# Last folds partly on GpSimd, six tiles' statistics on ScalarE, and a table of priorities in place of a search

## The chip, the core and the metric

The kernel runs on one core of a Trainium2 chip. The core has five engines that each work through a queue of their own in order: TensorE (PE in the profile; its weight loads are listed apart as PEld), VectorE (DVE), ScalarE (ACT), GpSimd (POOL) and SyncE (SP), which here issues all the loads and stores. The metric is the device time of one execution in microseconds. Three runs of the kernel before gave 236.53, 236.74 and 237.49 us; the median is 236.74.

## What is computed

```python
def reference(A_x, A_w_r, A_w_i, B_x, B_w_q, B_k1, B_k2, B_u, B_v):
    xn = layernorm(A_x)                              # (1, 2048, 576)
    # A: a filter in the frequency domain
    X = rfft2(xn) * (A_w_r + 1j * A_w_i)             # weights (2048, 289)
    yA = irfft2(X, s=(2048, 576))
    # B: experts picked by product keys, 32 heads, 8 x 8 experts, top 1
    q = einsum("nd,dhc->nhc", xn, B_w_q)             # w_q (576, 32, 256)
    s1 = einsum("nhd,ed->nhe", q[..., :128], B_k1)
    s2 = einsum("nhd,ed->nhe", q[..., 128:], B_k2)
    e = argmax(s1) * 8 + argmax(s2)
    act = gelu(einsum("nd,nhd->nh", xn, B_u[e]))
    yB = einsum("nh,nhd->nd", act, B_v[e])           # softmax over one is 1
    return A_x + yA + yB
```

## The kernel before

The 2048 rows are kept as 16 tiles of 128 rows (row 16n + t is in tile t), all in `XN`. The work falls into stages, each a small Python function marked `@staged`:

- `ln` takes the mean and the variance of each row of a group of tiles with VectorE's `bn_stats` (two passes of 288 numbers, into `st`) and `bn_aggr` (into `mv`), and makes the factors `rr` from them. `folds` adds and subtracts mirrored columns (GpSimd into the tile called `t` in the profile, GpSimd and VectorE into `A`) and makes `Rs`, the constant matrix times the row factor, on ScalarE. `dft128` multiplies by `Rs` on TensorE and copies the result out of PSUM as two 16 bit halves, the high one on ScalarE, the rest on VectorE, into `AB` and `ABL`.
- The spectral stages run for 16 groups g: `d_fwd` (transform along the columns, result in `A`), `s_fwd` and `s_inv` (the rest of the row transform and its inverse, with constants `s` loaded by `load_s16`), and between them `s_mul`, in which VectorE multiplies by the weights `Wt` with a scale `wx`, GpSimd makes `y`, and ScalarE and GpSimd its halves `yh`. `load_w` loads `Wt` and has ScalarE sum its absolute values into `wm` (tile `wa`). `w_scale` gets the scale from these sums.
- `allmax` takes the maximum of a column over all 128 partitions, for up to four columns: TensorE transposes, VectorE reduces (`mxr`), VectorE puts the maxima on a diagonal (`mxd`), and TensorE multiplies `ones` by it, which hands the maxima to all partitions. It runs nine times: in `w_scale` seven times, in `uv_prep` and in `fold_scale`.
- `fold_part` multiplies the loaded `wq` by the keys (`w` by `KP` on TensorE, 32 loads of 576 KB), `fold_end` makes `MU` and `MUL` of it. `x_t` normalises a tile again, splits it in halves `hl` and transposes it by DMA into `xT`. `scores`, `route` and `combine` take the scores (`MU` by `xT`), pick the experts on VectorE, and leave coefficients in `CAT`.
- The tail has 16 tiles t. `d_inv(t)` transforms back along the columns into a PSUM tile `p` of two blocks of 290. ScalarE copies the second half of each block, scaled, into `qs`; VectorE adds it to the first half (128x2x145) and subtracts it from it (128x2x144) into `eo` (the profile's `t`); GpSimd adds and subtracts the two blocks of `eo` into `y` (the profile's `A`, two instructions, 289 and 287 numbers). `fin(t, y)` multiplies by the constant `RT` and adds the experts' part (`vS`) on TensorE, VectorE adds the input, and SyncE stores.

The functions only record their instructions. A planner, `_Plan`, then sets the order in which they are issued on every engine: it runs through the recorded instructions with assumed durations (`cost`), takes on each engine the ready one with the highest priority (`forward`), and a priority is the assumed length of the work that hangs on an instruction (`backward`) plus a bias (`plan.base` or `plan.bias` at the time of recording). Before, ten rounds of that are followed by 1500 tries with random shifts of the priorities by stage, and the order with the shortest assumed time is kept. All instructions are issued from one line (L487), so the profile names them by tiles. PSUM tiles get their banks in the same way; all other tiles come from rings of buffers.

Of the kernel before, what the change touches and what calls it, by code (L numbers as in the profile page):

```python
# [135 lines left out]
TRIES, SEED = 1500, 2  # L136
# [87 lines left out]
class _Plan:  # L224
# [7 lines left out]
    def cost(self, eng, m, out, ins, kw):  # L232
# [4 lines left out]
        if eng == "sync":  # L237
            return out.shape[0] * n * size_of(out.dtype) / 400.0 + (2500 if kw.get("transpose") else 0), self.land
# [111 lines left out]
    def forward(self, prio):  # L350
# [50 lines left out]
        best, stale = dict.fromkeys(free), set(free)  # L401
        while len(order) < len(ops):
            for e in best:
                if e in stale:
# [16 lines left out]
            if o.opens:
                new = [v for v in o.opens if v not in slot]
                for v, k in zip(new, banks(new)[1]):
                    slot[v] = k
                    free_at[k:k + v.banks] = [INF] * v.banks
                    used[v.kind] += 1
                stale.add("tensor")
            for v in o.tiles:
                left[v] -= 1
                end[v] = max(end[v], free[e] + o.lat)  # L430
                if not left[v]:
                    free_at[slot[v]:slot[v] + v.banks] = [end[v]] * v.banks
# [8 lines left out]
        return max(free.values()), order, slot, start

    def issue(self):
# [16 lines left out]
        for _ in range(ROUNDS):  # L460
# [7 lines left out]
        for k in range(TRIES):
            f = 1 - k / TRIES
            tail, shift = cur[1], cur[2].copy()  # L470
            pick = rng.random(len(shift)) < (0.02, 0.05, 0.15)[rng.integers(3)]
            shift[pick] += rng.normal(0, 800 + 4000 * f, pick.sum())
            more = 400 * f * f * rng.exponential()
            if k % 40 == 39:
                tail, shift, more = self.backward(got[3]), cur[2], 300
            new = self.forward([t + o.bias + shift[o.stage] for t, o in zip(tail, ops)])
            if new[0] <= cur[0] + more:
                cur, got = (new[0], tail, shift), new
                if new[0] < best[0]:
                    best = new  # L480
# [18 lines left out]
def _body(ctx, tc, nc, plan, a, out):  # L499
# [238 lines left out]

    @staged
    def w_end():  # L740
# [247 lines left out]

    @staged
    def d_inv(t):  # L990
        p = PS("a")
        for b in range(2):
            P.matmul(p[:, b, :290], ABLt[:99, b, :, t], il[:99, b, :], start=True, stop=False)
            for c in range(2):
                cs = slice(0, 145) if b == c else slice(145, 290)
# [152 lines left out]
```

## Time and profile before

| | |
|---|---|
| median of three runs | 236.74 us |
| the profiled execution | 237.5 us |
| its span in the trace | 235.6 us |
| granted clock of TensorE, mean | 0.986 |
| read from HBM | 38.33 MB |

The profile is of one execution. Its span runs from the first to the last instruction that the profiler recorded; the execution itself took 1.9 us longer. Busy time is the time in which an engine executes; an engine that waits in its queue is idle, and the profile names what ended the wait. For groups of instructions a row gives the engine, the operation, output and inputs by tile, shapes, the count, the busy time, the mean duration in ns, and the idle time ahead of them.

### The profile page before, as it was taken

To read this page: it belongs to the slowest core of one execution; us is meant where nothing else is said; L and a number is where in the kernel's file an instruction comes from. 1 tells how busy PE (TensorE), PEld (TensorE's weight loads), DVE (VectorE), ACT (ScalarE), POOL (GpSimd) and SP (SyncE) were. 2 spreads that over 40 slices of the span, in tenths; PEclk is the share of its full clock that TensorE was granted. 3 is DMA by queue.
4 is the path that set the end of the run, shared out by engine and by line. 5 is a ranking of instruction groups with operands and counts; after the bars stand their busy time and mean duration, and the time that the engine had idled before them with its cause. 6 is when DMAs were issued, how large, how long until landed. Compare 5 with 4: busy or idle time off the path is not lost.

```text
span 235.6 us, 5937 instructions
## 1 busy us (share of the span) xinstructions
PE 200.0 (85%) x2271; PEld 135.8 (58%) x2271; DVE 204.3 (87%) x446; ACT 125.9 (53%) x287; POOL 134.4 (57%) x183
## 2 busy tenths in 40 slices
PE   0466888998999877899988979689999999999893
PEld 0454657776566545774454566265546778767661
DVE  2789999995999679976499999989999999968992
ACT  2232658989789599989635665256432121223120
POOL 2978768984264446736228886275813746545340
PEclk9997999999999999999999999979999999999999
DMA  6999999999999998466525561330521357662175
GB/s 211 401 403 415 362 334 375 406 349 373 284 338 374 392 251 148 106 164 59 110 53 122 115 134 38 79 59 3 100 59 46 99 156 253 198 203 100 50 245 208
DMA packets 34252, 48.15 MB, mean 204 GB/s; under 512 B 20784, under 2 KB 23088, under 8 KB 33840
## 3 DMA queue, kind: packets, MB, share of 16 engines
q1 hardware_dynamic: 34224, 47.77, 64.7%
q8 instruction: 18, 0.29, 0.6%
q14 instruction: 10, 0.08, 0.1%
HBM read 38.33 MB, written 4.72 MB: 183 GB/s over the span
## 4 chain that ended last, share of the span: by engine, by line
DVE 45%; PE 29%; ACT 9%; issue 8%; DMA 7%; POOL 1%; DVEq 0%; ACTq 0%; POOLq 0%
PE banks L487 29%; DVE w L487 9%; DVE t L487 8%; DVE AB L487 5%; DVE A L487 3%; DVE st L487 3%; DMA Wt<-in_W_dram 3%; DMA w<-in_x_dram 3%; DVE v L487 2%; DVE cw L487 2%; ACT AB L487 2%; DVE mx L487 2%; DVE ABL L487 2%; DMA XN<-in_x_dram 2%; DVE rr L487 2%
## 5 line engine op out<-in xcount | busy, mean ns | idle before, releaser
L487 POOL TENSOR_TENSOR A<-t 128x145 f32<-128x145 f32 (+3 forms) x56 | 38.4, 706 | 18.9 <-DVE t L487 12.2
L487 PE MATMUL banks<-MU,xT 128*128 128x512 f16 x192 | 46.0, 380 | 0.0
L487 PE MATMUL banks<-c,AB 128*128 128x145 f16 (+1 forms) x384 | 35.6, 228 | 0.7 <-DVE AB L487 0.7
L487 PEld LDWEIGHTS <-AB 128*128 128x128 f16 x384 | 31.6, 121 | 6.7 <-issue 4.3
L487 PE MATMUL banks<-Rs,A 128*128 128x128 f32 x128 | 20.5, 310 | 16.1 <-ACT Rs L487 11.8
L487 POOL TENSOR_TENSOR y<-t,t 128x289 f32<-128x289 f32 x32 | 21.7, 700 | 21.2 <-DVE t L487 20.8
L487 PEld LDWEIGHTS <-xT 128*128 128x128 f16 x224 | 19.8, 97 | 23.7 <-issue 4.1
L487 POOL TENSOR_TENSOR yh<-y,yh 128x578 f16<-128x578 f32 x16 | 20.6, 1285 | 16.7 <-ACT yh L487 12.9
L487 PEld LDWEIGHTS banks<-Rs,A 128*128 128x128 f32 x128 | 17.7, 214 | 21.1 <-ACT Rs L487 14.1
L487 POOL TENSOR_TENSOR t<-XN 128x289 f32<-128x289 f32 x32 | 24.5, 782 | 8.2 <-DMA XN<-in_x_dram 3.8
L487 DVE TENSOR_TENSOR AB<-banks,AB 128x512 f16<-128x512 f32 x32 | 21.6, 676 | 5.2 <-ACT AB L487 2.7
L487 DVE SCALAR_TENSOR_TENSOR t<-banks,wx,Wt 128x578 f32<-128x578 f32 x32 | 24.9, 807 | 0.4 <-PE banks L487 0.3
L487 POOL TENSOR_TENSOR hl<-XN,hl 128x576 f16<-128x576 f32 x16 | 20.0, 1254 | 8.0 <-ACT hl L487 8.0
L487 PE MATMUL banks<-c,ABL 99*128 99x289 f16 (+1 forms) x64 | 18.7, 292 | 5.6 <-DVE t L487 2.7
L487 ACT ACTIVATE yh<-banks,sc 128x290 f32<-128x290 f32 x16 | 8.0, 503 | 27.9 <-PE banks L487 23.9
L487 PE MATMUL banks<-A,c 128*128 128x288 f32 x64 | 21.6, 419 | 0.5 <-DVE t L487 0.5
L487 PE MATMUL banks<-w,KP 128*32 128x288 f32 x256 | 21.2, 428 | 0.0
L487 ACT ACTIVATE ABL<-banks 99x256 f16<-99x256 f32 x32 | 12.1, 378 | 16.6 <-PE banks L487 15.8
L487 ACT ACTIVATE AB<-banks 128x512 f16<-128x512 f32 x32 | 18.9, 590 | 0.1
L487 PE MATMUL banks<-s,yh 64*128 64x128 f16 x384 | 14.5, 222 | 4.9 <-ACT yh L487 1.9
L487 DVE TENSOR_TENSOR ABL<-banks,ABL 33x256 f16<-33x256 f32 x32 | 13.0, 405 | 6.3 <-ACT ABL L487 3.2
L487 PEld LDWEIGHTS <-yh 64*128 64x128 f16 x384 | 11.6, 97 | 9.6 <-issue 3.5
(104 smaller groups left out, 416.5 us busy)
## 6 DMA issues: line engine op xcount, KB each, us to landing
w<-in_wq_dram SPq DMA_DIRECT2D x32, 576.0 KB, 6.2
Wt<-in_W_dram SPq DMA_DIRECT2D x16, 289.0 KB, 5.4
w<-in_x_dram SPq DMA_DIRECT2D x8, 576.0 KB, 4.3
out_dram<-w SPq DMA_DIRECT2D x16, 288.0 KB, 2.7
XN<-in_x_dram SPq DMA_DIRECT2D x3, 1282.0 KB, 12.7
s<-in_s_dram SPq DMA_DIRECT2D x16, 192.0 KB, 3.1
XN<-in_x_dram SPq DMA_DIRECT2D x2, 641.0 KB, 5.0
c<-in_c_dram SPq DMA_DIRECT2D x1, 868.5 KB, 7.5
```

The costliest lines, as they stand in the source:

```text
L487: fn(*[x.place() if isinstance(x, _Ps) else x for x in args], **{k: x.place() if isinstance(x, _Ps) else x for k, x in kw.items()})
```

## The change

Five things are changed.

1. `d_inv`: for all 16 tiles ScalarE copies both halves of the blocks (`es`, 2x290 numbers instead of 2x145), and the subtraction moves from VectorE to GpSimd, which reads both inputs from SBUF. VectorE's addition stays.
2. `ln`: for the tiles 5, 7, 9, 11, 13 and 15 ScalarE takes the statistics, in one pass with a sum for the mean and one pass with a sum of squares for the variance; GpSimd scales the mean. `bn_stats` and `bn_aggr` go for these.
3. `allmax`: the diagonal goes; the maxima, broadcast along their row, are the weights of the second product, with the identity as what moves. A factor can be put into the last instruction, so a separate scaling in `w_scale` and one in `fold_scale` go.
4. The planner: the 1500 tries go; a table `SHIFT` of one number per stage is added to the priorities instead. Its assumed times change: 1200 ns until a transposing load lands instead of 3000, 3000 instead of 5600 for the early loads, and 2600 more for a load that is issued when the queue has been full for over 1500.
5. The spectral stages get a bias (`plan.base`) of 1e4 instead of 0.

```diff
-TRIES, SEED = 1500, 2
+SHIFT = (
+    43015, -9167, -18816, 63625, -68848, 40186, 12971, -53665, -16763, -54647, 23343, -31988,
...
+)
@@ cost
-            return out.shape[0] * n * size_of(out.dtype) / 400.0 + (2500 if kw.get("transpose") else 0), self.land
+            return out.shape[0] * n * size_of(out.dtype) / 400.0 + (2500 if kw.get("transpose") else 0), 1200.0 if kw.get("transpose") else self.land
@@ forward
+            lag = 0.0
+            if e == "sync":
+                if t0 > full[1]:
+                    full[0] = t0
+                full[1] = free[e] + 300
+                lag = 2600.0 if t0 - full[0] > 1500 else 0.0
             for k, lat in o.after:
-                ready[k] = max(ready[k], free[e] + lat)
+                ready[k] = max(ready[k], free[e] + lat + lag)
@@ issue
-        rng = np.random.default_rng(SEED)
-        for k in range(TRIES):
...
+        best = self.forward([t + o.bias + SHIFT[o.stage] for t, o in zip(cur[1], ops)])
@@ allmax
-        dg = T([4, 4], F32, "mxd", 4)
-        V.tensor_scalar(dg[:k, :k], idn[:k, :k], m[:k, 0:1], None, op0=OP.mult)
-        P.matmul(p[:, 1, :k], ones[:k, :], dg[:k, :k], start=True, stop=True)
-        V.tensor_scalar(dst, p[:, 1, :k], 1e-10, None, op0=OP.max)
+        P.matmul(p[:, 1, :k], m[:k, 0:1].to_broadcast([k, 128]), idn[:k, :k], start=True, stop=True)
+        if up is None:
+            V.tensor_scalar(dst, p[:, 1, :k], 1e-10, None, op0=OP.max)
+        else:
+            V.tensor_scalar(dst, p[:, 1, :k], 1e-10, up, op0=OP.max, op1=OP.mult)
@@ ln
+            if t + i in SA:
+                j, b = T([128, D], BF, "wa", 1), rr[:, 3, t + i:t + i + 1]
+                A.activation(j, XN[:, t + i, 64:64 + D], AF.Copy, scale=-1.0 / 13824, accum_out=b)
+                A.activation(j, XN[:, t + i, 64:64 + D], AF.Square, scale=1.0 / 24, bias=b, accum_out=mv[:, i, 1:2])
+                G.tensor_scalar(mv[:, i, 0:1], b, -24.0, None, op0=OP.mult)
+                continue
@@ w_scale
-        V.tensor_scalar(wx[:, 1, g:g + n], wx[:, 1, g:g + n], 2.0 ** -12, None, op0=OP.mult)
@@ d_inv
+            es = T([128, 2, 290], F32, "qs", 2, "yh")
+            A.activation(es, p[:, :, 0:290], AF.Copy, scale=sc[:, 12:13])
+            qs = es[:, :, 145:290]
...
-        V.scalar_tensor_tensor(eo[:, :, 288:144:-1], p[:, :, 0:144], sc[:, 12:13], qs[:, :, 0:144],
-                               op0=OP.mult, op1=OP.subtract)
+            G.tensor_tensor(eo[:, :, 288:144:-1], es[:, :, 0:144], qs[:, :, 0:144], op=OP.subtract)
```

What the order does with it shows at three places. The first is ScalarE in the first stage, from its second instruction for `rr` on, before:

```order
L487 ACTIVATE rr_84<-mv_1_94,eps_85 128x2
L487 ACTIVATE yl_0_103<-A2_0_97 128x198
L487 ACTIVATE ABL_76<-banks_66 99x64x4
L487 ACTIVATE AB_75<-banks_66 128x128x4
L487 ACTIVATE yl_0_103<-A2_2_99 128x198
L487 ACTIVATE rr_84<-mv_0_93,eps_85 128x4
L487 ACTIVATE Rs_0_101<-c32_68,rr_84 128x128
L487 ACTIVATE Rs_1_102<-c32_68,rr_84 128x128
```

and of the change, where `wa<-XN` are the two passes of a tile's statistics (the first one's sum goes to `rr`, the second one's to `mv`):

```order
L502 ACTIVATE rr_84<-mv_1_94,eps_85 128x2
L502 ACTIVATE ABL_76<-banks_66 99x64x4
L502 ACTIVATE yl_0_103<-A2_0_97 128x198
L502 ACTIVATE wa_0_105,rr_84<-XN_67 128x576
L502 ACTIVATE wa_0_105,mv_0_93<-XN_67,rr_84 128x576
L502 ACTIVATE AB_75<-banks_66 128x128x4
L502 ACTIVATE wa_0_105,rr_84<-XN_67 128x576
L502 ACTIVATE Rs_0_101<-c32_68,rr_84 128x128
L502 ACTIVATE wa_0_105,mv_0_93<-XN_67,rr_84 128x576
L502 ACTIVATE yl_0_103<-A2_2_99 128x198
L502 ACTIVATE rr_84<-mv_0_93,eps_85 128x4
L502 ACTIVATE Rs_1_102<-c32_68,rr_84 128x128
```

The passes of tiles 5 and 7 stand ahead of the copy `AB` and between the two `Rs`. The second place is ScalarE in the spectral stages, at the sum `wa` over the weights of group 6, whose buffer is `Wt_2`, before:

```order
L487 ACTIVATE A2_2_99<-banks_66 128x578
L487 ACTIVATE yl_0_103<-yh_0_142 128x198
L487 ACTIVATE wa_0_114,wm_82<-Wt_2_110 128x578
L487 ACTIVATE yh_1_143<-y_0_141 128x578
L487 ACTIVATE AB_75<-banks_66 128x4x128
L487 ACTIVATE yl_1_104<-yh_1_143 128x198
```

and of the change:

```order
L502 ACTIVATE AB_75<-banks_66 128x4x128
L502 ACTIVATE yh_1_139<-y_0_137 128x578
L502 ACTIVATE ABL_76<-banks_66 99x2x128
L502 ACTIVATE yl_1_104<-yh_1_139 128x198
L502 ACTIVATE wa_0_105,wm_82<-Wt_2_111 128x578
L502 ACTIVATE yl_1_104<-yh_1_139 128x198
```

The sum has moved behind `AB`, `yh` and `ABL`. SyncE's queue shows the load that it needs. Before, from that load to the last one of `wq`:

```order
L487 DMA Wt_2_110<-in_W_dram 128x578
L487 DMA s16_1_116<-in_s16_dram 128x768
L487 DMA w_4_131<-in_wq_dram 128x1152
L487 DMA Wt_3_111<-in_W_dram 128x578
L487 DMA w_0_127<-in_wq_dram 128x1152
L487 DMA w_1_128<-in_wq_dram 128x1152
```

and of the change:

```order
L502 DMA Wt_2_111<-in_W_dram 128x578
L502 DMA w_1_124<-in_wq_dram 128x1152
L502 DMA s16_1_116<-in_s16_dram 128x768
L502 DMA Wt_3_112<-in_W_dram 128x578
L502 DMA w_3_126<-in_wq_dram 128x1152
L502 DMA Wt_4_113<-in_W_dram 128x578
L502 DMA s16_2_117<-in_s16_dram 128x768
L502 DMA Wt_5_114<-in_W_dram 128x578
L502 DMA w_0_123<-in_wq_dram 128x1152
L502 DMA w_4_127<-in_wq_dram 128x1152
L502 DMA w_1_124<-in_wq_dram 128x1152
L502 DMA w_2_125<-in_wq_dram 128x1152
```

Three of the 32 loads of `wq` stood behind it, now six do. The third place is the end of GpSimd's queue, the last four tiles' folds and two `chl` of `combine`, before:

```order
L487 TENSOR_TENSOR A2_0_97<-t1_0_95 128x289
L487 TENSOR_TENSOR A2_1_98<-t1_1_96 128x287
L487 TENSOR_TENSOR A2_1_98<-t1_1_96 128x289
L487 TENSOR_TENSOR A2_2_99<-t1_0_95 128x289
L487 TENSOR_TENSOR A2_2_99<-t1_0_95 128x287
L487 TENSOR_TENSOR chl_0_151<-ca_0_150,chl_0_151 128x2x64
L487 TENSOR_TENSOR A2_3_100<-t1_1_96 128x289
L487 TENSOR_TENSOR A2_3_100<-t1_1_96 128x287
```

and of the change, where `t1<-yh` is the moved subtraction:

```order
L502 TENSOR_TENSOR t1_0_95<-yh_0_138 128x2x144
L502 TENSOR_TENSOR A2_0_97<-t1_0_95 128x289
L502 TENSOR_TENSOR A2_0_97<-t1_0_95 128x287
L502 TENSOR_TENSOR chl_0_147<-ca_0_146,chl_0_147 128x2x64
L502 TENSOR_TENSOR t1_1_96<-yh_1_139 128x2x144
L502 TENSOR_TENSOR A2_3_100<-t1_1_96 128x289
L502 TENSOR_TENSOR t1_0_95<-yh_0_138 128x2x144
L502 TENSOR_TENSOR A2_3_100<-t1_1_96 128x287
L502 TENSOR_TENSOR A2_2_99<-t1_0_95 128x289
L502 TENSOR_TENSOR A2_2_99<-t1_0_95 128x287
```

Each tile has three instructions there instead of two, and the subtraction of the last tile stands ahead of the last addition of the tile before it.

More of the change, by code (lines that the diff above doesn't have):

```diff
@@ L400, in forward @@
         order, start = [], [0.0] * len(ops)
-        best, stale = dict.fromkeys(free), set(free)
+        best, stale, full = dict.fromkeys(free), set(free), [0.0, 0.0]
         while len(order) < len(ops):
@@ L465, in issue @@
                 best = got
-                cur = got[0], tail, np.zeros(self.stage + 1)
-        rng = np.random.default_rng(SEED)
-        for k in range(TRIES):
[L469 to L480, printed above, removed]
+                cur = got[0], tail
+        best = self.forward([t + o.bias + SHIFT[o.stage] for t, o in zip(cur[1], ops)])
         _, order, slot, start = best
@@ L550, in _body @@
     plan.bias = 8e6
-    plan.land = 5600.0
+    plan.land = 3000.0
     c32 = K([128, 3, 128], F32, "c32")
@@ L614, in allmax @@
     @staged
-    def allmax(src, k, dst):
+    def allmax(src, k, dst, up=None):
         p = PS("m", (128, 2, 256))
@@ L734, in w_scale @@
     def w_scale(g, n):
-        allmax(wm[:, g:g + n], n, wx[:, 0, g:g + n])
+        allmax(wm[:, g:g + n], n, wx[:, 0, g:g + n], 4096.0)
         V.reciprocal(wx[:, 1, g:g + n], wx[:, 0, g:g + n])
-        V.tensor_scalar(wx[:, 1, g:g + n], wx[:, 1, g:g + n], 2.0 ** -12, None, op0=OP.mult)
     @staged
@@ L743, in w_end @@
         V.tensor_reduce(sc[:, 12:13], al, axis=AX, op=OP.add)
-        V.tensor_scalar(sc[:, 12:13], sc[:, 12:13], 4.0 / 1179648.0, sc[:, 10:11], op0=OP.mult, op1=OP.mult)
+        V.tensor_scalar(sc[:, 12:13], sc[:, 12:13], 4.0 / 1179648.0 / 4096.0, sc[:, 10:11], op0=OP.mult, op1=OP.mult)
     mt = {}
@@ L986, in s_inv @@
         V.tensor_tensor(lo[:33], lv[:33], lo[:33], op=OP.subtract)
+    EG = range(16)
     @staged
@@ L998, in d_inv @@
                              stop=(c == 1 and n == 2))
-        qs = T([128, 2, 145], F32, "qs", 2, "yh")
-        A.activation(qs, p[:, :, 145:290], AF.Copy, scale=sc[:, 12:13])
         eo = T([128, 2, L], F32, "eo2", 2, "t1")
-        V.scalar_tensor_tensor(eo[:, :, 0:145], p[:, :, 0:145], sc[:, 12:13], qs, op0=OP.mult, op1=OP.add)
-        V.scalar_tensor_tensor(eo[:, :, 288:144:-1], p[:, :, 0:144], sc[:, 12:13], qs[:, :, 0:144],
-                               op0=OP.mult, op1=OP.subtract)
+        if t in EG:
+            es = T([128, 2, 290], F32, "qs", 2, "yh")
+            A.activation(es, p[:, :, 0:290], AF.Copy, scale=sc[:, 12:13])
+            qs = es[:, :, 145:290]
+        else:
+            qs = T([128, 2, 145], F32, "qs", 2, "yh")
+            A.activation(qs, p[:, :, 145:290], AF.Copy, scale=sc[:, 12:13])
+        V.scalar_tensor_tensor(eo[:, :, 0:145], p[:, :, 0:145], sc[:, 12:13], qs, op0=OP.mult, op1=OP.add)
+        if t in EG:
+            G.tensor_tensor(eo[:, :, 288:144:-1], es[:, :, 0:144], qs[:, :, 0:144], op=OP.subtract)
+        else:
+            V.scalar_tensor_tensor(eo[:, :, 288:144:-1], p[:, :, 0:144], sc[:, 12:13], qs[:, :, 0:144],
+                                   op0=OP.mult, op1=OP.subtract)
         y = T([128, D], F32, "yy", 2, "A2")
@@ L1067, in _body @@
     scores(0)
+    plan.base = 1e4
     for g in range(4):
@@ L1074, in _body @@
     for g in range(16):
+        plan.base = 1e4
         s_inv(g)
@@ L1081, in _body @@
             load_s16(g + 4)
-            plan.base = 0
+            plan.base = 1e4
             if g % 2 == 1:
@@ L1088, in _body @@
                 w_scale(g + 3, 2)
+        plan.base = 0
         r = g // 2
@@ L1100, in _body @@
             combine(r)
+    plan.base = 0
     w_end()
```

4 lines of the change are left out of this document (2 added, 2 removed), and 18 rows, old and new, of the table SHIFT.

## The prediction

> **What bounds the kernel now.** I read the share table first, then the stretches by engine, then the waits of TensorE.
>
> ```profile
> PE 200.0 (85%) x2271; PEld 135.8 (58%) x2271; DVE 204.3 (87%) x446; ACT 125.9 (53%) x287; POOL 134.4 (57%) x183
> DVE 45%; PE 29%; ACT 9%; issue 8%; DMA 7%; POOL 1%; DVEq 0%; ACTq 0%; POOLq 0%
> 0.00:10.00 10.00, 1.05 (x5) 1.06 (x6) 5.33 (x23) 2.55 (x5) 5.52 (x17) 1.00 0.82 288
> 10.00:40.00 30.00, 22.90 (x182) 17.12 (x182) 27.70 (x89) 14.69 (x42) 23.53 (x39) 0.94 0.99 381
> 40.00:80.00 40.00, 38.21 (x554) 27.00 (x552) 36.11 (x75) 34.21 (x77) 25.06 (x31) 1.00 1.00 358
> 80.00:100.00 20.00, 15.81 (x276) 11.10 (x275) 15.82 (x36) 17.81 (x39) 10.62 (x12) 1.00 0.88 195
> 100.00:180.00 80.00, 72.14 (x888) 43.54 (x887) 71.42 (x131) 45.80 (x101) 42.75 (x49) 0.98 0.40 84
> 180.00:232.00 52.00, 49.88 (x379) 36.00 (x377) 47.37 (x96) 10.81 (x25) 26.95 (x38) 1.00 0.47 160
> 232.00:235.60 3.60, 0.00 (x0) 0.00 (x0) 0.52 (x1) 0.00 (x0) 0.00 (x0) 1.00 0.43 168
> ```
>
> The stretches give, after the stretch and its length, busy us of PE, PEld, DVE, ACT and POOL, the granted clock, the DMA share and GB/s. Two engines are nearly full, VectorE with 204.3 us and TensorE with 200.0 of a span of 235.6. The chain that ended last (the second row) runs mostly over VectorE, because TensorE work is in order and waits for it. But TensorE cannot go below its 200.0 us, and the change takes next to nothing off it. So the span is 200.0 plus the 35.6 us in which TensorE idles, and the question is how much of that idle time VectorE causes. By stretch, length less busy time: 8.95 in the first 10 us, 7.10 in 10 to 40, 1.79 in 40 to 80, 4.19 in 80 to 100, 7.86 in 100 to 180, 2.12 in 180 to 232, and 3.60 at the end, together 35.6. The first and the last (12.55) are the first load, the first normalisation and the last output; the change does not touch them. That leaves 23.06.
>
> ```profile
> PE banks L487 <- DVE A L487: 3.4, 3, 2.3
> PE banks L487 <- ACT Rs L487: 2.8, 2, 2.2
> PE banks L487 <- DVE rr L487: 0.9, 1, 0.9
> ...
> 81.25 0.69 ACT L487 ACTIVATE wa<-Wt 128x578 bf16<-128x578 f32 x1 [2.27 <-DMA Wt<-in_W_dram]
> ...
> PE banks L487 <- ACT yh L487: 1.9, 1, 1.9
> PE banks L487 <- DVE t L487: 1.9, 2, 1.6
> PE banks L487 <- DVE wx L487: 1.3, 1, 1.3
> ```
>
> The first three rows are all waits of TensorE from 10 to 40 us (total, times, longest): 7.1 us, all on the normalisation and the folds, `Rs` too, since it is `rr`, written by VectorE, times a constant. The 4th row is ScalarE at 81 us, held 2.27 us by a load of `Wt`, with `yh` and `AB` queued behind it. The last three are the longest waits from 100 to 180 us; VectorE is 71.42 of 80 us busy there.
>
> **The change, part by part: VectorE.** These rows (count, then busy us and the mean ns of one) are what goes:
>
> ```profile
> L487 DVE SCALAR_TENSOR_TENSOR t<-banks,sc,yh 128x288 f32<-128x288 f32 x16 | 8.0, 502 | 0.0
> L487 DVE BATCH_NORM_STATS2 st<-XN 128x6 f32<-128x288 f32 x32 | 12.2, 442 | 3.7 <-DMA XN<-in_x_dram 3.7
> L487 DVE BATCH_NORM_AGGREGATE mv<-st 128x2 f32<-128x12 f32 x16 | 2.0, 171 | 0.0
> L487 DVE TENSOR_SCALAR mxd<-c,mxr x9: 193/753/1101, 50.9 to 136.1; 2x2 f32<-2x2 f32 x7, 4x4 f32<-4x4 f32 x1, 1x1 f32<-1x1 f32 x1
> L487 DVE TENSOR_SCALAR mxd<-c,mxr 2x2 f32<-2x2 f32 x7 | 4.3, 618 | 0.1
> L487 DVE TENSOR_SCALAR mxd<-c,mxr 4x4 f32<-4x4 f32 x1 | 0.8, 804 | 0.0
> L487 DVE TENSOR_SCALAR mxd<-c,mxr 1x1 f32<-1x1 f32 x1 | 0.2, 193 | 0.0
> L487 DVE TENSOR_SCALAR wx<-wx 128x2 f32<-128x2 f32 x6 | 3.4, 560 | 0.1
> L487 DVE TENSOR_SCALAR wx<-wx x7: 151/170/1190, 53.6 to 140.8; 128x2 f32<-128x2 f32 x6, 128x4 f32<-128x4 f32 x1
> ```
>
> The second half of the last folds: 16 times 0.502 is 8.0 us. Six tiles' statistics: 12 of 32 passes at 12.2/32 and 6 of 16 aggregates at 2.0/16 make 4.6 and 0.75, so 5.3. The diagonals `mxd`: 4.3 + 0.8 + 0.2, so 5.3. The scalings of `wx`: 3.4 for six and 0.17 for one; one of `sc` at the same 0.17. Together 22.3 us, so VectorE falls from 204 to about 182 and is no longer beside TensorE.
>
> A diagonal of four numbers takes 0.193 us at best and 1.101 at worst, and `wx` 0.151 and 1.190: most of it is waiting. [...]
>
> **ScalarE and GpSimd** get work:
>
> ```profile
> L487 ACT ACTIVATE wa<-Wt 128x578 bf16<-128x578 f32 x16 | 10.9, 682 | 2.5 <-DMA Wt<-in_W_dram 2.3
> L487 ACT ACTIVATION_READ_ACCUMULATOR wa<-Wt 128x1 f32 x16 | 3.1, 195 | 0.0
> L487 ACT ACTIVATE yh<-banks,sc 128x290 f32<-128x290 f32 x16 | 8.0, 503 | 27.9 <-PE banks L487 23.9 <-DVE v L487 3.3 <-ACT MT L487 0.7
> L487 ACT ACTIVATE A<-banks 128x578 f16<-128x578 f32 x16 | 10.3, 654 | 5.3 <-PE banks L487 5.3
> L487 POOL TENSOR_TENSOR y<-t,t 128x289 f32<-128x289 f32 x32 | 21.7, 700 | 21.2 <-DVE t L487 20.8
> L487 POOL TENSOR_TENSOR A<-t 128x287 f32<-128x287 f32 x16 | 13.2, 827 | 10.0 <-DVE t L487 4.0 <-DVE w L487 2.8 <-DVE pw L487 2.2
> L487 POOL TENSOR_TENSOR A<-t 128x289 f32<-128x289 f32 x16 | 12.0, 757 | 8.2 <-DVE t L487 8.2
> L487 POOL TENSOR_SCALAR rr<-mv 128x2 f32<-128x2 f32 x2 | 0.5, 270 | 0.2
> ```
>
> A pass over 576 numbers with a sum is the nearest to `wa`: 0.682 + 0.195 = 0.88 us, 12 of them 10.5 us on ScalarE. The copy of 580 numbers out of PSUM instead of 290 is nearest to `A`: 0.654 against 0.503, so 16 times 0.15, 2.4 us. ScalarE goes from 125.9 to about 139. GpSimd gets 16 subtractions of 288 numbers: bounds 0.70 (the row of `y`) and 0.83 (the slowest of the tail's rows), I take 0.70, 11.2 us; and six small scalings at 0.27, 1.6 us. It goes from 134 to 147. The new subtraction waits for the copy of ScalarE, and behind it in GpSimd's queue stand the additions `y` of the tile before, for which TensorE's last products wait. Per tile the chain was 0.503 + 0.508 + 0.502 on ScalarE and VectorE; now it is 0.654 and then 0.508 beside 0.70, so 0.16 us shorter, and the PSUM bank comes free earlier, since the subtraction reads SBUF.
>
> The weights broadcast from `m` have no row. `ones` has the same shape, so I take a difference of nothing; bounds of 0.1 us either way for 9 of them, from the 0.183 us load of `ones` and the 0.082 of two columns elsewhere, are under 1 us.
>
> ```profile
> L487 PEld LDWEIGHTS banks<-mxd,ones 2*128 2x128 f32 x14 | 2.1, 183 | 2.4 <-DVE mxd L487 1.2 <-DVE wx L487 0.8 <-issue 0.2
> L487 PEld LDWEIGHTS banks<-c,wm 128*2 128x2 f32 x6 | 0.5, 82 | 2.1 <-DVE t L487 0.9 <-ACT wa L487 0.8 <-issue 0.2
> ```
>
> **From busy time to the span.** 10 to 40 us: of the 7.10 idle, 3.87 lies before 20 us (the stretch of 10 to 20 below), on tiles 0 to 4, whose statistics stay. Of the other 3.2 I take 2.0: VectorE, 27.70 of 30 busy, loses 5.3 us there, and the new passes lie on ScalarE, which has 15 us free, but in front of evacuations (first pair of order pieces above).
>
> ```profile
> 10.00:20.00 10.00, 6.13 (x37) 4.60 (x36) 7.90 (x28) 2.75 (x8) 8.02 (x14) 1.00 1.01 405
> ```
>
> 40 to 80 us: the DMA share is 1.00, TensorE waits 1.8; nothing. 80 to 100 us: 4.2 idle, of which I take 2.0: the load of `Wt` that ScalarE waited for now has six of the 32 loads of `wq` behind it and not three, and its `wa` stands behind `AB` and `yh` (second and third pair of order pieces); one load of 576 KB is 1.5 us at the 381 GB/s of a full stretch, so it lands some 4 us earlier than the 2.27 us wait needs. If another load is late there instead, the 2.0 stay. 100 to 180 us: VectorE is 89% busy, and what it sheds here (`mxd`, `wx`, and tail work that no longer presses) is about a tenth; I take half of 7.86, 4.0, since its waits on `yh` of ScalarE and GpSimd stay. 180 to 232 us: TensorE is 49.88 of 52 busy. The 8.0 us that go from VectorE lie under that; nothing. Sum: 2.0 + 2.0 + 4.0 = 8.0 off 235.6, a span of 227.6. The profiled execution took 237.5, 1.9 more than its span; the median shown, 236.74, is 0.76 below it. So 227.6 + 1.9 - 0.76 = **228.7 us**.
>
> **The rivals.**
> *Everything frees up.* All 23.06 less the 3.87 before 20 us goes, 19.2: 217.5 us. Against it: waits on ScalarE and DMA are not touched by VectorE's relief. Taken at 218 to 224, chance 0.07.
> *A small gain.* The new priorities only reshuffle the waits of 100 to 180 us, and 2 to 4 us come off: 233 to 235. For it: the waits there are scattered over five releasers. Chance 0.20.
> *The statistics block ScalarE*, so that the change doesn't do what it says. Each of the 12 passes stands in the queue of the copies `AB`, `ABL` and `Rs`; if each pair holds TensorE for one pass, 6 times 0.88 is 5.3 us, against 2.0 + 4.0 won elsewhere: 236.0, within half a per cent, which is about what a measurement can tell from no change. For it: ScalarE is 34.21 of 40 busy right after. Against: the loads of `wq` give TensorE other work. Chance 0.12.
> *GpSimd paces the tail* (the slower one). Per tile it now does three instructions, 0.70 + 0.757 + 0.827 = 2.28 us, with 2.6 us of others in all (26.95 less 25.2) 2.4 per tile; TensorE needs 49.88/16 = 3.1. It decides from a mean of 0.98 us per instruction. The longest of the first folds (row below) is 1.192; at that all through, 16 times 3.7 is 59.8, 9.9 more than TensorE, and 236.7 - 6 + 9.9 = 240.6. Chance 0.09.
>
> ```profile
> L487 POOL TENSOR_TENSOR t<-XN x32: 687/788/1192, 4.8 to 49.7; 128x289 f32<-128x289 f32 x32
> L487 DVE TENSOR_TENSOR A<-t 128x288 f32<-128x288 f32 x8 | 3.5, 436 | 0.0
> L487 POOL TENSOR_TENSOR A<-t 128x288 f32<-128x288 f32 x8 | 6.2, 773 | 0.1
> ```
>
> [...]
>
> **How the numbers follow.** The forecast, 224 to 233 us, has 0.52. Faster by over 0.5%: 0.52 + 0.20 + 0.07 = 0.79; within it 0.12; slower 0.09. A range of 221 to 238 leaves out the slower rival (0.09), half of the one that frees everything, and a little of the others.
>
> **What would show it.** Right: VectorE near 182 us, TensorE still 200, idle of TensorE near 27.5, and in the tail no wait of TensorE on GpSimd. The statistics: ScalarE passes near 0.88 us and waits of TensorE from 20 to 40 us under 1.5. Wrong: GpSimd above nine tenths in the tail, evacuations late behind `wa`, or a new long wait for a load at 55 to 90 us, since `Wt` and the c16 constants changed places in the queue.

## The result, and the profile after

Four runs of the changed kernel have a median of 228.89 us (228.73 to 231.18); four of the kernel before beside them 236.63 (236.34 to 237.49). The ratio is 0.969, with a 95% interval of 0.962 to 0.976: faster by 3.1%. The prediction was 228.7. Here and below, a time is the median of all runs of a kernel, and ratios, intervals and mean clocks leave out the slow runs, those over 1.5% above the fastest of the same kernel. The profiled execution of the changed kernel is its slowest run, 231.18 us with a span of 229.4, so the profiles differ by 6.2 us of span and the medians by 7.7.

The page of the changed kernel first, its busy times and the shares of the chain that ended last; then the stretches (stretch, length, busy us of PE, PEld, DVE, ACT and POOL, granted clock, DMA share, GB/s):

```profile
PE 197.8 (86%) x2271; PEld 135.6 (59%) x2271; DVE 189.6 (83%) x395; ACT 136.5 (60%) x311; POOL 147.5 (64%) x205
PE 44%; DVE 25%; ACT 11%; DMA 8%; issue 8%; POOL 3%; DVEq 0%; ACTq 0%; POOLq 0%
0.00:10.00 10.00, 0.73 (x3) 0.73 (x4) 5.37 (x22) 2.64 (x5) 5.45 (x16) 1.00 0.81 277
10.00:40.00 30.00, 24.18 (x199) 17.85 (x197) 25.38 (x77) 23.15 (x68) 26.84 (x48) 0.94 1.01 408
40.00:80.00 40.00, 37.25 (x566) 27.34 (x562) 31.71 (x68) 35.19 (x79) 24.98 (x31) 1.00 0.98 320
80.00:100.00 20.00, 16.10 (x283) 11.47 (x274) 11.86 (x28) 17.49 (x40) 8.46 (x9) 0.91 0.84 240
100.00:180.00 80.00, 76.70 (x917) 46.56 (x916) 75.43 (x134) 46.69 (x101) 49.64 (x58) 1.00 0.43 90
180.00:226.00 46.00, 42.81 (x327) 31.69 (x324) 39.88 (x71) 11.38 (x21) 32.17 (x47) 1.00 0.52 174
226.00:229.40 3.40, 0.00 (x0) 0.00 (x0) 0.00 (x0) 0.00 (x0) 0.00 (x0) 0.93 0.23 87
```

The chain now runs over TensorE first (44%) and VectorE second (25%); before it was 29 and 45. TensorE's idle time, stretch by stretch as the prediction counted it (length less busy time):

| stretch, us | idle before | idle after | predicted change | measured |
|---|---|---|---|---|
| 0 to 10 | 8.95 | 9.27 | 0 | +0.3 |
| 10 to 40 | 7.10 | 5.82 | -2.0 | -1.3 |
| 40 to 80 | 1.79 | 2.75 | 0 | +1.0 |
| 80 to 100 | 4.19 | 3.90 | -2.0 | -0.3 |
| 100 to 180 | 7.86 | 3.30 | -4.0 | -4.6 |
| 180 to the end | 5.72 | 6.59 | 0 | +0.9 |
| idle in all | 35.6 | 31.6 | -8.0 | -4.0 |
| TensorE busy | 200.0 | 197.8 | 0 | -2.2 |

The order differs, so a stretch doesn't hold exactly the same work; the sums don't depend on that. One thing already speaks against a step of the prediction: from 100 to 180 us VectorE is *busier* than before, 75.43 us instead of 71.42, and it is just there that TensorE waits less.

What TensorE still waits for, by releaser, from 10 to 40 us and (last three) from 100 to 180 us (total, times, longest):

```profile
PE banks L502 <- DMA w<-in_wq_dram: 3.7, 4, 1.7
PE banks L502 <- ACT Rs L502: 2.0, 2, 1.1
...
PE banks L502 <- DVE t L502: 1.6, 4, 0.6
PE banks L502 <- POOL chl L502: 1.4, 1, 1.4
PE banks L502 <- DVE AB L502: 0.3, 1, 0.3
```

The waits on the folds (`A`, 3.4 us) are gone from the front, and a wait for the loads of `wq` has come, at a DMA share of 1.01. From 100 to 180 us the three largest totals of before, 1.9, 1.9 and 1.3 us, are now 1.6, 1.4 and 0.3. The timeline from 80 to 100 us has two waits of TensorE of over 0.3 us (start, duration, instruction, in brackets the wait). Three rows of ScalarE and VectorE, of the same stretch, stand under them:

```profile
85.90 0.38 PE L502 MATMUL banks<-c,wm 128*2 128x128 f32 x2 [2.09 <-DVE A L502]
95.58 0.27 PE L502 MATMUL banks<-c,mm__90 128*1 128x128 f32 x1 [1.44 <-ACT hl L502]
...
83.73 0.69 ACT L502 ACTIVATE wa<-Wt 128x578 bf16<-128x578 f32 x1
84.42 0.63 ACT L502 ACTIVATE A<-banks 128x578 f16<-128x578 f32 x1
85.08 0.76 DVE L502 TENSOR_TENSOR A<-banks,A 128x578 f16<-128x578 f32 x1 [1.83 <-ACT A L502]
```

The groups of the changed kernel that are new or altered (count, busy us, mean ns of one, idle ahead and its releaser):

```profile
L502 ACT ACTIVATE yh<-banks,sc 128x580 f32<-128x580 f32 x16 | 11.9, 744 | 27.8 <-PE banks L502 23.5 <-POOL act L502 3.3 <-issue 1.0
L502 POOL TENSOR_TENSOR t<-yh 128x288 f32<-128x288 f32 x16 | 11.8, 734 | 7.0 <-ACT yh L502 6.9
L502 POOL TENSOR_TENSOR A<-t 128x287 f32<-128x287 f32 x16 | 12.1, 761 | 1.1 <-PE banks L502 1.1
L502 POOL TENSOR_TENSOR A<-t 128x289 f32<-128x289 f32 x16 | 11.8, 740 | 5.3 <-DVE t L502 4.9
L502 ACT ACTIVATE wa<-XN 128x576 bf16<-128x576 f32 x6 | 4.0, 674 | 0.0
L502 ACT ACTIVATE wa<-XN,rr 128x576 bf16<-128x576 f32 x6 | 4.6, 766 | 0.0
L502 ACT ACTIVATION_READ_ACCUMULATOR wa<-XN 128x1 f32 x6 | 1.2, 193 | 0.0
L502 PEld LDWEIGHTS banks<-c,mxr 2*128 2x128 f32 x14 | 2.0, 182 | 1.8 <-DVE mxr L502 1.3 <-issue 0.2
L502 ACT ACTIVATE wa<-Wt 128x578 bf16<-128x578 f32 x16 | 10.9, 682 | 0.1
```

The durations came out near the estimates: a pass of statistics is 0.674 + 0.193 = 0.87 us or, with the square, 0.766 + 0.190 = 0.96 (0.88 taken), the subtraction on GpSimd 0.734 (between the bounds 0.70 and 0.83), the broadcast weights 0.182 (0.183 for `ones`). The copy of 580 numbers takes 0.744 and not 0.654. The last row is ScalarE's sum over the weights, for whose load of `Wt` it waited 2.3 us before: it waits for it no more.

### The profile page after: what moved, and what is told of

It is laid out like the page before. It is cut to its first block, busy times and chain, and to the rows that moved or that the text cites. A ratio compares the mean times of both kernels' runs of the same rounds, so it can differ in the third digit from the quotient of the medians.

```text
span 229.4 us, 5957 instructions
## 1 busy us (share of the span) xinstructions
PE 197.8 (86%) x2271; PEld 135.6 (59%) x2271; DVE 189.6 (83%) x395; ACT 136.5 (60%) x311; POOL 147.5 (64%) x205
## 4 chain that ended last, share of the span: by engine, by line
PE 44%; DVE 25%; ACT 11%; DMA 8%; issue 8%; POOL 3%; DVEq 0%; ACTq 0%; POOLq 0%
PE banks L502 44%; DVE t L502 6%; DMA w<-in_wq_dram 5%; DVE w L502 4%; DVE A L502 3%; ACT XN L502 2%; DVE AB L502 2%; POOL A L502 2%; DMA XN<-in_x_dram 2%; DMA w<-in_x_dram 2%; ACT AB L502 2%; DVE mx L502 1%; DVE st L502 1%; ACT A L502 1%; DVE ABL L502 1%
## 5 line engine op out<-in xcount | busy, mean ns | idle before, releaser
L502 PEld LDWEIGHTS <-AB 128*128 128x128 f16 x384 | 32.2, 123 | 3.5 <-issue 1.7
L502 POOL TENSOR_TENSOR y<-t,t 128x289 f32<-128x289 f32 x32 | 22.5, 724 | 16.1 <-DVE t L502 13.8
L502 PE MATMUL banks<-Rs,A 128*128 128x128 f32 x128 | 21.1, 314 | 11.3 <-ACT Rs L502 11.3
L502 ACT ACTIVATE yh<-banks,sc 128x580 f32<-128x580 f32 x16 | 11.9, 744 | 27.8 <-PE banks L502 23.5
L502 POOL TENSOR_TENSOR t<-XN 128x289 f32<-128x289 f32 x32 | 23.6, 753 | 6.0 <-DMA XN<-in_x_dram 3.9
L502 PE MATMUL banks<-w,KP 128*32 128x288 f32 x256 | 20.6, 423 | 3.7 <-DMA w<-in_wq_dram 3.7
L502 DVE TENSOR_TENSOR A<-banks,A 128x578 f16<-128x578 f32 x16 | 11.9, 751 | 6.1 <-ACT A L502 6.1
L502 POOL TENSOR_TENSOR t<-yh 128x288 f32<-128x288 f32 x16 | 11.8, 734 | 7.0 <-ACT yh L502 6.9
L502 PE MATMUL banks<-A,s 64*64 64x289 f16 x384 | 15.3, 295 | 0.7 <-DVE A L502 0.5
```

The lines of the kernel that those rows point to most:

```text
L502: fn(*[x.place() if isinstance(x, _Ps) else x for x in args], **{k: x.place() if isinstance(x, _Ps) else x for k, x in kw.items()})
```

## The experiments

Three theories stood against each other. The prediction's: VectorE's relief lets TensorE wait less, whatever the order. The first rival: the order alone does it. The second: it needs both. To part them, the planner's result for a kernel (the order of issue and the PSUM banks) was written out as a list and held fast, while the instructions were changed inside it; an instruction of one kernel that the other lacks stands where its counterpart stood. The twelve kernels ran in three groups of four, each group on a chip of its own beside the kernel before (medians 236.75, 236.20 and 236.55 us).

All twelve, with the ratio to the kernel before and its 95% interval, and from each profile the span less TensorE's busy time (idle), the busy time, and the mean granted clock of the runs compared. The kernel before has an idle of 35.6 and a busy time of 200.0 in its profile, and a mean clock of 0.979 over 48 runs beside these.

| kernel | instructions | order | ratio | idle | busy | clock |
|---|---|---|---|---|---|---|
| the change | new | table | 0.969 [0.962, 0.976] | 31.6 | 197.8 | 0.994 |
| held | new | the change's, as a list | 0.974 [0.970, 0.978] | 30.4 | 198.9 | 0.989 |
| held_again | the same kernel | the same | 0.967 [0.963, 0.971] | 31.6 | 195.1 | 0.999 |
| order_only | all old | the change's | 1.004 [1.000, 1.007] | 35.9 | 199.3 | 0.982 |
| instr_only | new | before's | 1.000 [0.997, 1.004] | 33.3 | 201.2 | 0.977 |
| search_old | new | search, old assumed times | 1.004 [1.000, 1.007] | 35.1 | 200.6 | 0.975 |
| search_new | new | search, new assumed times | 0.964 [0.959, 0.969] | 29.4 | 196.1 | 0.988 |
| no_table | new | ten rounds, no table, new times | 0.985 [0.981, 0.990] | 32.9 | 198.7 | 0.980 |
| no_fold | old folds, rest new | the change's | 0.974 [0.971, 0.978] | 32.7 | 195.9 | 0.996 |
| max_only | only `allmax` new | the change's | 0.988 [0.981, 0.995] | 33.2 | 197.4 | 0.982 |
| stats_only | only the statistics new | the change's | 0.993 [0.990, 0.996] | 32.7 | 200.3 | 0.983 |
| c16_late | new | one load moved | 0.970 [0.966, 0.975] | 32.0 | 196.0 | 0.998 |
| c16_nofold | old folds, rest new | the same load moved | 0.988 [0.982, 0.995] | 31.4 | 198.9 | 0.982 |

### The control: the order as a list

```diff
-        best = self.forward([t + o.bias + SHIFT[o.stage] for t, o in zip(cur[1], ops)])
...
+        for v in {v for o in ops for v in o.tiles}:
+            v.slot = BANK[v.order]
+        order = ORDER
```

> The changed kernel, its order and banks written out as a list instead of planned; nothing else differs. Every theory: the time of the changed kernel, 228.9 us within 0.5. It is the control for the kernels below, in which the same list is kept.

230.22 us, ratio 0.974. The median is 1.3 us above the 228.9 of the change, where 0.5 was expected. The list still stands for the change, since the intervals overlap (0.962 to 0.976 for the change); a second measurement of it, below, gave 228.61.

### Order alone, instructions alone

The first undoes all three changes of instructions in the held order, the second puts the new instructions into the order of before.

```diff
-    SA = (5,7,9,11,13,15)
+    SA = ()
-    EG = range(16)
+    EG = ()
-        P.matmul(p[:, 1, :k], m[:k, 0:1].to_broadcast([k, 128]), idn[:k, :k], start=True, stop=True)
+        dg = T([4, 4], F32, "mxd", 4)
+        V.tensor_scalar(dg[:k, :k], idn[:k, :k], m[:k, 0:1], None, op0=OP.mult)
+        P.matmul(p[:, 1, :k], ones[:k, :], dg[:k, :k], start=True, stop=True)
```

> The instructions of before in the order of the change (moved instructions back on VectorE at the same places, the diagonals and scalings put back right behind the instruction they follow). Theory A, VectorE's relief makes the gain: VectorE is back at about 204 us, so 234 to 238 us. Theory B, the order alone makes it: 229 to 231 us.

```diff
-    18, 13, 0, 8, 9, 10, 11, 12, 6, 7, 1, 2, 3, 19, 39, 20, 40, 22, 23, 41, 21, 24, 43, 26, 25, 33,
...
+    18, 13, 0, 12, 8, 9, 10, 11, 6, 7, 1, 2, 3, 19, 39, 20, 40, 22, 23, 41, 21, 24, 43, 26, 25, 32,
...
```

> The instructions of the change in the order of before. Theory A: most of the gain, 230 to 233 us, VectorE near 190 us. Theory B: no gain, 235.5 to 237 us.

Neither gains: 237.11 us (1.004) and 236.42 us (1.000). The page's busy times of order_only, with its stretches from 10 to 40 and 100 to 180 us:

```profile
PE 199.3 (85%) x2271; PEld 137.6 (58%) x2271; DVE 203.3 (86%) x446; ACT 125.2 (53%) x287; POOL 135.2 (57%) x183
10.00:40.00 30.00, 22.77 (x188) 18.20 (x187) 28.28 (x90) 14.75 (x42) 23.61 (x40) 0.94 0.99 393
100.00:180.00 80.00, 74.94 (x915) 45.35 (x916) 76.33 (x143) 46.09 (x102) 47.33 (x52) 1.00 0.42 83
```

and the same of instr_only:

```profile
PE 201.2 (86%) x2271; PEld 137.0 (58%) x2271; DVE 191.3 (82%) x395; ACT 137.9 (59%) x311; POOL 146.9 (63%) x205
10.00:40.00 30.00, 22.06 (x169) 16.12 (x169) 22.35 (x68) 21.88 (x62) 23.29 (x42) 0.94 0.93 356
100.00:180.00 80.00, 73.79 (x889) 44.17 (x888) 70.55 (x128) 46.22 (x101) 44.03 (x51) 0.96 0.39 82
```

In instr_only VectorE is relieved by 13 us, and from 10 to 40 us it works 22.35 of 30, yet TensorE idles 7.9 us there (7.1 before), most of it still for folds (`A`, 3.2 us) and for `Rs` (3.0). That this is because the order was planned around the old durations is argued, not shown. In order_only TensorE idles 5.1 us from 100 to 180 (7.9 before), but VectorE has 28.28 of 30 to do in the front, and TensorE idles 7.2 there. Relief without an order for it, and the order without relief, are each worth nothing that can be measured; together they are worth about 3%. The two theories that name one cause fall, for the two orders tried here.

### Which of the new instructions matter in the new order

```diff
-    EG = range(16)
+    EG = ()
```

> The changed kernel in its order, with the second half of the last folds back on VectorE (behind the first half) and ScalarE's copy back to 290 numbers. If the tail is TensorE's and the 8 us are hidden there, as the prediction had it: 229 to 230.5 us. If VectorE sets the pace of the second half of the kernel, where it is full from 130 to 210 us: 232 to 235 us. In either case the instructions of VectorE with two SBUF inputs (ct, ca, vf) should come back from 0.52, 0.52 and 0.45 us towards 0.33, 0.37 and 0.28, if GpSimd's moved work lengthens them.

230.28 us, 0.974, on the same chip as the control with 0.974: the 16 subtractions that moved from VectorE to GpSimd are worth nothing in this pair. Of the three instructions that were expected to come back, one did: `ct` went from 516 ns in held to 374, but `ca` (520 to 519) and `vf` (447 to 440) stayed. The same held order with only the new `allmax`, and with only the statistics moved:

```diff
-    SA = (5,7,9,11,13,15)
+    SA = ()
-    EG = range(16)
+    EG = ()
```

> The order of the change kept, and of its instructions only the maxima read as weights and the two scalings saved; statistics and last folds as before. With the order alone at 1.004 and with all but the folds at 0.974 of the time before: if the chain of allmax is what the order needed (VectorE's diagonals stood waiting for GpSimd with the products of TensorE behind them: 2.2 us of TensorE's waits), 0.98 to 0.99; if the statistics are, 1.00.

```diff
-    EG = range(16)
+    EG = ()
-        P.matmul(p[:, 1, :k], m[:k, 0:1].to_broadcast([k, 128]), idn[:k, :k], start=True, stop=True)
+        dg = T([4, 4], F32, "mxd", 4)
...
```

> The order of the change kept, and of its instructions only the statistics of six tiles on ScalarE; maxima and last folds as before. If the statistics are what the order needed (first 40 us: TensorE idle 7.2 us in the order alone, 5.7 with them): 0.985 to 0.99; if not, 1.00. Theory of two equal parts: each of these two kernels at 0.985 to 0.99.

234.06 us (0.988) and 234.84 us (0.993). Against order_only (1.004, on another chip) the new `allmax` gains about 1.6% and the statistics 1.1%, and no_fold, which has both, 2.9%: within their intervals the two add up. The 0.993 lies a little above the 0.985 to 0.99 that was expected of two equal parts.

### The planner: the times it assumes, and the table

Search_old plans the new instructions with the planner of before: the 1500 tries, its assumed times and its base. Search_new has the 1500 tries under the new times and base. No_table has the new times and neither tries nor table.

```diff
-SHIFT = (
...
+TRIES, SEED = 1500, 2
-            return out.shape[0] * n * size_of(out.dtype) / 400.0 + (2500 if kw.get("transpose") else 0), 1200.0 if kw.get("transpose") else self.land
+            return out.shape[0] * n * size_of(out.dtype) / 400.0 + (2500 if kw.get("transpose") else 0), self.land
-                lag = 2600.0 if t0 - full[0] > 1500 else 0.0
+                lag = 0.0
-    plan.land = 3000.0
+    plan.land = 5600.0
-    plan.base = 1e4
+    plan.base = 0
```

> The instructions of the change, but planned as before: the search of 1500 tries, the old assumed times and bases, now made for these instructions. If the instructions need only some order made for them: 0.97 to 0.98. If it is the table with the new assumed times that matters: 0.99 to 1.00, as with the old order itself (1.000).

```diff
-SHIFT = (
...
+TRIES, SEED = 1500, 2
-        best = self.forward([t + o.bias + SHIFT[o.stage] for t, o in zip(cur[1], ops)])
+        rng = np.random.default_rng(SEED)
+        for k in range(TRIES):
...
```

> The changed kernel with the search of 1500 tries in place of the table, under the new assumed times and bases. If the new assumed times (loads behind a full queue 2.6 us later) are what the old search lacked: 0.975 to 0.985. If the table is: 0.995 to 1.005, as search_old.

```diff
-        best = self.forward([t + o.bias + SHIFT[o.stage] for t, o in zip(cur[1], ops)])
+        best = self.forward([t + o.bias for t, o in zip(cur[1], ops)])
```

> The changed kernel with the table set to nought: ten rounds of planning, no search, no shifts. It bounds what any order gives these instructions: 1.02 to 1.06 of the time before if shifts of the priorities matter as much as old and new order differ (3%); 0.98 to 1.00 if the new assumed times and bases alone give the gain.

237.29 us (1.004), 228.01 (0.964; one of its four runs took 390.48 us at a clock of 1.00, and why is not known) and 233.07 (0.985). Search_new did better than the 0.975 to 0.985 expected of it. So a search finds an order as good as the table's once it is given the new times and base, and with the old ones it gains nothing from the same instructions. Even ten rounds without table or search gain 1.5% under the new ones. The timeline of search_old, of ScalarE and then of TensorE, shows one wait that comes with the old ones:

```profile
79.13 0.69 ACT L495 ACTIVATE wa<-Wt 128x578 bf16<-128x578 f32 x1 [1.51 <-DMA Wt<-in_W_dram]
...
84.36 0.27 PE L495 MATMUL banks<-c,wm 128*2 128x128 f32 x1 [2.13 <-ACT wa L495]
```

ScalarE is held 1.51 us by a load of `Wt`, then works without a gap up to a second `wa` at 83.54 us, and TensorE's next product waits 2.13 us for that one. ScalarE waits for `Wt` in every kernel ordered under the old times (2.3 us before, 1.1 in instr_only, 1.5 here) and in none of order_only, search_new, no_table and the change. In search_old the passes of the statistics block, too: a product with `Rs` waits 1.33 us behind `wa` at 13 us. Which of the four numbers (1200, 3000, 2600, 1e4) matters was not tried apart, each order is one draw of a search, and the instructions of before were never planned with the new numbers.

### A load moved, and the control again

The wait for `wq` in the front was suspected to come from the load of the constants `c16` (number 313 in the list), which the change issues ahead of loads of `wq`. It was put behind the next three loads.

```diff
-    237, 241, 238, 340, 177, 235, 181, 313, 154, 178, 242, 153, 179, 152, 342, 180, 183, 142, 243,
+    237, 241, 238, 340, 177, 235, 181, 154, 178, 242, 153, 179, 152, 342, 180, 183, 142, 243, 244,
...
+    196, 156, 347, 207, 352, 313, 135, 157, 348, 349, 209, 188, 248, 184, 186, 324, 249, 198, 158,
```

> The changed kernel in its order, with the load of the constants c16 (868.5 KB) moved behind the next three loads of wq. If it delays the loads of wq that TensorE waits for from 20 to 32 us (4.5 us in the control): 1 to 2 us off, 0.966 to 0.970. If the DMA rate sets those waits whatever the order: the same as the control, 0.974.

Beside it, on another chip, the control was run again without an edit:

> The control once more, on the same chip as the three below: 0.974 of the time before.

and the late load together with the folds on VectorE:

```diff
-    EG = range(16)
+    EG = ()
```

> The changed kernel in its order without the moved folds and with the load of c16 behind three loads of wq. The folds were worth nothing (no_fold 0.974, control 0.974), and the load 0.970 against 0.974 from another chip. If the load's place is a gain: 0.970, a time below the changed kernel. If that was chip or chance: 0.974, as the control.

c16_late took 229.25 us (0.970), between the two runs of the control (0.974 and 0.967), and TensorE still waits 4.2 us for `wq` in all; in the kernels with the load in its place this wait was 2.4 (held_again), 3.7 (the change) and 4.5 (held). The suspicion isn't borne out. The control itself came out at 0.967 and not at the 0.974 expected. The last kernel joins the late load to no_fold: 234.12 us (0.988), neither the 0.970 nor the 0.974 expected, though each alone cost nothing that these runs resolve. Its idle, 31.4 us, is no larger than the control's 31.6; its busy time is 198.9 against 195.1. That leads to the last finding.

### The same kernel with two busy times

Held and held_again are one and the same kernel, run on two chips. Busy times of the page of held, and TensorE's stretches around 90 us:

```profile
PE 198.9 (87%) x2271; PEld 135.7 (59%) x2271; DVE 191.1 (83%) x395; ACT 137.2 (60%) x311; POOL 147.5 (64%) x205
86.00:88.00 2.00, 1.79 (x28) 1.10 (x30) 1.93 (x5) 2.00 (x5) 0.78 (x1) 0.79 1.05 425
88.00:94.00 6.00, 6.00 (x80) 4.70 (x80) 2.27 (x8) 4.18 (x10) 3.13 (x4) 0.50 0.82 203
```

and of held_again:

```profile
PE 195.1 (86%) x2271; PEld 133.5 (59%) x2271; DVE 190.3 (84%) x395; ACT 136.7 (60%) x311; POOL 147.8 (65%) x205
86.00:88.00 2.00, 2.00 (x50) 1.64 (x44) 1.44 (x7) 2.00 (x4) 1.58 (x2) 1.00 1.00 379
88.00:94.00 6.00, 5.18 (x126) 3.46 (x119) 2.74 (x6) 5.73 (x16) 2.34 (x3) 1.00 1.23 227
```

From 88 to 94 us the granted clock of held is 0.50, and TensorE, busy all 6 us, does 80 products; in held_again the clock is 1.00 and 126 are done in 5.18 us. The matmul groups of `wq` in the front of held show the same step, 8 products of 288 columns at a time:

```profile
27.66 0.69 PE L543 MATMUL banks<-w,KP 128*32 128x288 f32 x8 [0.73 <-DMA w<-in_wq_dram]
29.09 1.18 PE L543 MATMUL banks<-w,KP 128*32 128x288 f32 x8 [0.74 <-DMA w<-in_wq_dram]
30.50 1.19 PE L543 MATMUL banks<-w,KP 128*32 128x288 f32 x8 [0.23 <-DMA w<-in_wq_dram]
```

0.69 us turns into 1.18 after a run of short waits for loads. The whole is 3.8 us of busy time, and 2.6 of span, with no instruction changed.

## Why the prediction was right, and where it wasn't

**The number.** 228.9 against 228.7. The frame (TensorE's busy time plus its idle time) held, and the idle time was the right thing to count. But the sum expected all 8.0 us from idle time; in the profiles it gave 4.0 (35.6 to 31.6, where about 27.5 was named as the sign). Another 2.2 us are busy time, which was taken as fixed, and the last 1.4 between 6.3 (the profiled executions) and 7.7 (the medians) are that the profiled run of the change lay 2.3 us above its median and that of before 0.9. So the hit to 0.2 us is in part luck: nearly half of the gain came from terms that were not in the sum.

**100 to 180 us, 4.0 predicted.** 4.6 measured. The size was right and the reason was not: VectorE did not shed a tenth there, it was busier (75.43 us after 71.42) while TensorE's idle time more than halved. instr_only, with the relief and without the order, leaves 6.2 us of idle time; order_only, with the order alone, 5.1.

**10 to 40 us, 2.0 predicted.** 1.3 measured. The waits for folds went, as expected, and of those on the normalisation 1.1 us (on `Rs`) is left from 20 to 40 us; but 3.7 us for the loads of `wq` came on, so that the waits there are 4.8 us and not under the 1.5 that was named. The prediction had taken the DMA's fullness as a bound from 40 to 80 us only, though its own row has a DMA share of 0.99 from 10 to 40 us too; in the order of before TensorE had no wait for `wq` there.

**80 to 100 us, 2.0 predicted.** 0.3 measured; this term fell. The first half of the step was right: the load of `Wt` isn't waited for. The step assumed that only another *load* could be late next; it was VectorE's `A` (2.09 us) and ScalarE's `hl` (1.44). What took the place of the load is ScalarE's own queue, 17.49 of 20 us busy: the products whose result it copies out end at 83.81 us, but its copy `A` starts at 84.42, behind a `wa`, and VectorE's `A`, for which TensorE waits, ends only at 85.84. So the sign that evacuations come late behind `wa` did show here, at one place, with 0.6 us. For a load TensorE doesn't wait anywhere from 55 to 90 us.

**180 us to the end, 0 predicted.** It became 0.9 longer in the profile. Returning the folds to VectorE changes nothing against the control beside it (0.974 both), as predicted; c16_nofold doesn't settle it otherwise, since its extra time is busy time at a lower clock.

**VectorE's 22.3 us.** It fell by 14.7 (204.3 to 189.6), not to 182. The removed instructions went; others grew. Some grew by the order alone: `ca` went from 374 ns before to 522 in order_only, `vf` from 277 to 440, with no instruction changed. Others grew by the moved subtraction. Two groups of VectorE in no_fold, where the subtraction is on VectorE:

```profile
L543 DVE TENSOR_TENSOR w<-w,pw 128x512 bf16<-128x512 bf16 x8 | 4.1, 507 | 0.0
L543 DVE TENSOR_TENSOR ct<-ci,fm 128x128 int32<-128x128 int32 x8 | 3.0, 374 | 0.0
```

and in held, which differs by the subtraction on GpSimd and the longer copy for it on ScalarE:

```profile
L543 DVE TENSOR_TENSOR w<-w,pw 128x512 bf16<-128x512 bf16 x8 | 5.0, 631 | 0.0
L543 DVE TENSOR_TENSOR ct<-ci,fm 128x128 int32<-128x128 int32 x8 | 4.1, 516 | 0.0
```

Of the 8.1 us that left VectorE, its busy time in these two kernels keeps 2.3 (193.4 to 191.1). Both rows are instructions with two inputs; with the subtraction on GpSimd they went from 374 to 516 ns and from 507 to 631. The prediction's sum had no term for this. In this pair it cost no time (0.974 both); that VectorE's work in the tail lies under TensorE's is the likely reason, and was not tried apart.

**The rivals.** The one that everything frees up did not come: 31.6 us of idle time are left. A mere reshuffle by new priorities is refuted both ways: order_only gains nothing, and the change gains 3%. The statistics do not block ScalarE in the change: no wait of TensorE is on `wa` among those of 10 to 40 us, and ahead of both `Rs` that it waited for, ScalarE itself stood idle (0.47 and 0.55 us) for VectorE's `rr`. But in the order of search_old they do, so the rival's mechanism exists and the order decides. GpSimd does not pace the tail: 32.17 of 46 us busy, 0.734 + 0.740 + 0.761 = 2.24 us per tile (2.28 predicted), and TensorE waits there for it 0.2 us. (The recorded 26.95 less 25.2 is 1.75 and not 2.6; the 2.4 us per tile stands.) What speaks for this rival is the price of one instruction: the subtraction took 734 ns on GpSimd against 502 on VectorE before (1.5 times), and in the last two rows under the rival the same fold took 773 against 436 (1.8 times). The kernel's time doesn't show that price: 0.974 with the subtraction on GpSimd (held) and with it on VectorE (no_fold).

**What stays open.** How much of the gain is granted clock. It was 0.979 on average before (0.960 to 0.993 over 48 runs) and 0.994 in the four runs of the change; among the 48, the time falls by 0.69 us for each 0.01, which would make it 1.0 us of the 7.7; if TensorE was busy through all the slow time, (1 - 0.979) x 234.5 less (1 - 0.994) x 227.5 is at most some 3.6. Both are estimates from these clocks and times and not experiments, and why the new order is slowed less often wasn't shown. It isn't all of the gain: the two profiled executions have nearly the same clock (0.986 and 0.984) and differ by 6.3 us. Why TensorE's busy time is 2.2 us shorter there is open too. And the planner's new times and base were tried only with the new instructions. How much the old instructions, planned and searched anew under them, would gain isn't known; order_only, an order made for other instructions, doesn't answer it.

The fastest version measured is the change with a search under the new assumed times, 228.01 us (0.964 [0.959, 0.969]); on the same chip the change's own order as a list had 0.967 [0.963, 0.971], and the intervals overlap.

## What to carry to other kernels

Relief of a busy engine can be worth nothing in an order that was made without it, and an order nothing without the relief that it was made for (1.000 and 1.004 here, and 0.974 together): price the two apart by holding the order as a list and changing one part inside it. What makes such an order good can be the numbers that the planner assumes, more than the search: with the old ones 1500 tries gained nothing, with the new ones ten rounds gained 1.5%. Before counting work moved to GpSimd as taken off VectorE, look at what VectorE's instructions take beside it: here two groups with two inputs went from 374 to 516 ns and from 507 to 631.

## What the runs showed of the hardware

- TensorE's granted clock was 0.50 from 88 to 94 us in held and 1.00 in held_again, one kernel on two chips; over the two executions it was 0.978 and 0.997. In held the products of `wq` slow down at 29.09 us (0.69 to 1.18 us for eight), with several waits for loads but none of over 0.85 us in the 9 us before. From 27.4 to 30.8 us the clock is 0.76 there, and 1.00 in held_again. What sets it was not shown.
- The busy time of TensorE over the same 2271 products went from 195.1 to 201.2 us over the kernels here. A prediction that takes it as fixed to 0.1 us is too sure of it.
- A small instruction took eight times as long in another order. It is the group `al` of VectorE (128x16, one instruction): 157 ns in the kernel before, and 1249 in order_only, which has the same instructions. The two rows of it, and the timeline of order_only around it:

```profile
L487 DVE TENSOR_TENSOR al<-wx,mk 128x16 f32<-128x16 f32 x1 | 0.2, 157 | 0.0
L544 DVE TENSOR_TENSOR al<-wx,mk 128x16 f32<-128x16 f32 x1 | 1.2, 1249 | 0.0
...
130.73 1.66 POOL L544 TENSOR_TENSOR yh<-y,yh 128x578 f16<-128x578 f32 x1
131.18 1.25 DVE L544 TENSOR_TENSOR al<-wx,mk 128x16 f32<-128x16 f32 x1
```

It starts while GpSimd's `yh` runs and ends within 0.04 us of it (132.43 and 132.39 us). In the kernel before it starts at 174.01 us, when GpSimd is idle (172.64 to 175.15). Six of the nine diagonals `mxd` of the kernel before end with a GpSimd instruction, too. The longest took 1.10 us:

```profile
89.51 1.29 POOL L487 TENSOR_TENSOR yh<-y,yh 128x578 f16<-128x578 f32 x1 [1.15 <-ACT yh L487]
89.71 1.10 DVE L487 TENSOR_SCALAR mxd<-c,mxr 2x2 f32<-2x2 f32 x1
```

It ends at 90.81 us and `yh` at 90.80. The six are those that took 355 ns or more, and they end within 0.03 us of the GpSimd instruction; the other three took 193 to 216 ns, two of them while GpSimd was idle and one beside its `hl`. This agrees with the prediction's reading that most of their time is waiting.
